# Second batch's sums over positions: from TensorE to VectorE, and two query loads issued earlier

## The chip, the cores and the metric

The kernel runs on one core of a Trainium2 chip. The metric is the device time of one execution in microseconds (us). A core has TensorE (PE, matrix multiply; its weight loads are shown apart as PEld), VectorE (DVE), ScalarE (ACT), GpSimd (POOL) and SyncE (SP), whose queue issues every load and store of this kernel. Each engine works through its own list of instructions in order, and waits where an instruction needs something from another engine or from a load.

## What is computed

An attention with keys and values that are averaged over groups of 8 positions, then two feed-forward layers over the 4608 tokens (8 batches of 576 positions; 8 heads of 64):

```
k_p = k.reshape(B, H, Sp, 8, D).mean(axis=3)      # 576 positions -> 72
v_p = v.reshape(B, H, Sp, 8, D).mean(axis=3)
attn = softmax(q @ k_p.T / sqrt(D));  x = attn @ v_p
h = x @ w_in;  x = (h * sigmoid(1.702 * h)) @ w_out       # 512 -> 2048 -> 512
out = ((x @ w_a) * (x @ w_b)) @ w_out2                    # 512 -> 1536 -> 512
```

The sums over 8 positions (the means, with the factor put elsewhere) are what the change moves.

## The kernel before, in words

**Tiling.** The 4608 tokens are 36 units of 128 tokens, and 9 blocks of 512 tokens (4 units each). A batch has 4.5 units, so units 0 to 3 need batch 0 alone, unit 4 needs batches 0 and 1, units 5 to 7 batch 1. Attention of a unit `u` has four stages: `stage_b1` (scores `sc` on PE from queries `q` and the block-diagonal keys `kbd`, maximum `mx` on DVE, exponentials `at` on ACT, in two halves), `stage_b2` (`sm`, `at` scaled, DVE), `stage_c` (transposes `pt` on PE, copied to `aT` by ACT) and `stage_d` (`px` = values times `aT` on PE, split into `xhi` on ACT, line 85, and `xlo` on DVE, line 86).

**Feed-forward.** Every large product is made of three matmuls of 512 columns (`mm3`, lines 130 to 132) on operands split in a high and a low part. One step of the first layer for a slice `f` of the hidden width is `emit_h` (12 matmuls into `h`; then `g` by ACT and DVE, `ghi` by ACT, `glo` by DVE, line 400) and `emit_y` (12 matmuls into `acc`). The weights of a slice are loaded raw (`raw`) and converted by DVE with ACT (`convert`, lines 108 to 127), in four parts for a slice.

**The start.** Block 0's attention (units 0 to 3) is written in a fixed DVE order by `in_order`, which puts each operation behind the newest DVE operation; the parts of the weights of slices 0 and 1 are placed between. Then come the first `FA` = 6 slices of layer 1 on block 0 (steps 0 to 5). Around them `filler` places, in a fixed DVE order too, the conversions of slices 2 to 5 and the attention of units 4 to 7 (the list `ahead_`). After these the loop over all remaining steps runs, with the later attention and weights spread over it.

**Where the sums are made.** Batch 0's: `sum_k` (line 194; DVE adds up, ACT writes `kbd` by `to_kbd`) and `sum_v` (line 214; DVE). Batch 1's: `sum_k_pe` (line 200) and `sum_v_pe` (line 219) on PE, as products with the identity matrix, 8 for each half, added up in PSUM (`ksp`, `vsp`); ACT writes `kbd` from `ksp`, and copies `vsp` to `vs` (line 229). Their places are lines 627 to 628 (keys, behind step 0's `emit_h`) and 635 to 637 (values, behind step 0's `emit_y`). Batches 2 and on use `sum_k` and `sum_v`.

**What sets the order.** On DVE the fixed order of `in_order`. On the other engines a scheduler orders the instructions when the program is built, by its own estimate of when the inputs are there. The loads of the start (lines 575 to 591) go out on SP in the order in which they are written; `qs` holds the queries of units 0 to 3, `kvraw` the keys and values of batches 0 and 1.

Of the kernel before, what the change touches and what calls it, by code (L numbers as in the profile page):

```python
# [9 lines left out]
F32 = mybir.dt.float32  # L10
# [6 lines left out]
POOL = 8  # L17
# [7 lines left out]
def tile_kernel(ctx, tc, q, k, v, w_in, w_out, w_a, w_b, w_o2, out):  # L25
# [13 lines left out]
    nc = tc.nc  # L39
    P = 128  # L40
    NU, _, NP, _ = q.shape
    B, SP, H, D, _ = v.shape
# [19 lines left out]
    ps = ctx.enter_context(tc.tile_pool(name="ps", bufs=4, space=bass.MemoryType.PSUM))  # L62
# [7 lines left out]
    def vec(made):  # L70
        newest[0] = made.ins
        return made

    def in_order(*ops):

        for o in ops:
            if newest[0] is None:
                o()
            else:
                with tc.issue_after(newest[0]):  # L80
                    o()
# [52 lines left out]
    ident = const.tile([P, P], F32, name="ident")  # L134
# [22 lines left out]
    ap_ = at.enter_context(tc.tile_pool(name="ap", bufs=1))  # L157
# [4 lines left out]
    q_t, ks_t, vs_t, at_t, atT_t, kraw_t, vraw_t = {}, {}, {}, {}, {}, {}, {}  # L162
# [10 lines left out]
    def load_q(u, t=None):  # L173
        q_t[u] = ap_.tile([P, NP, P], F32, tag="q", name="q", bufs=2) if t is None else t
        nc.sync.dma_start(out=q_t[u], in_=q[u])
# [11 lines left out]
    def to_kbd(b, half, ks):  # L187


        cs = slice(2 * half, 2 * half + 2)  # L190
        nc.scalar.mul(out=kbd[b % 2][0:D, cs, 0:SP], in_=ks[0:D], mul=scale)
        nc.scalar.mul(out=kbd[b % 2][D:P, cs, SP:2 * SP], in_=ks[D:P], mul=scale)
# [4 lines left out]
        vec(nc.vector.tensor_reduce(out=ks, in_=raw, op=ALU.add, axis=AX.X))  # L197
        to_kbd(b, half, ks)

    def sum_k_pe(b, half):  # L200

        ks = ps.tile([P, 2, SP], F32, tag="ps", name="ksp")
        raw = kraw_t.pop((b, half)).rearrange("p c (s r) -> p c s r", r=POOL)
        for r in range(POOL):
            nc.tensor.matmul(out=ks, lhsT=ident, rhs=raw[:, :, :, r], start=r == 0, stop=r == POOL - 1)
        to_kbd(b, half, ks)

    def load_v(b, h, n, raw=None):
        if raw is None:
            raw = ap_.tile([SP, n, D, POOL], F32, tag="vraw", name="vraw", bufs=2)  # L210
        nc.sync.dma_start(out=raw, in_=v[b, :, h:h + n])
        vraw_t[b, h] = raw

    def sum_v(b, h, n):
        if h == 0:
            vs_t[b] = ap_.tile([SP, H, D], F32, tag="vs", name="vs", bufs=2)
        vec(nc.vector.tensor_reduce(out=vs_t[b][:, h:h + n, :], in_=vraw_t.pop((b, h)), op=ALU.add, axis=AX.X))

    def sum_v_pe(b, h, n):

        if h == 0:
            vs_t[b] = ap_.tile([SP, H, D], F32, tag="vs", name="vs", bufs=2)
        raw = vraw_t.pop((b, h))
        vp = ps.tile([SP, n, D], F32, tag="ps", name="vsp")
        for r in range(POOL):
            nc.tensor.matmul(  # L226
                out=vp, lhsT=ident[:SP, :SP], rhs=raw[:, :, :, r], start=r == 0, stop=r == POOL - 1
            )
        nc.scalar.copy(out=vs_t[b][:, h:h + n, :], in_=vp)

    def stage_b1(u, half):
        qT = q_t[u]
# [68 lines left out]
    def op(f, *a):  # L301
        return lambda: f(*a)
# [30 lines left out]
    def as_words(t):  # L333
        return t.rearrange("p (f w) -> p f w", w=2)

    def sources(key):
        kind, f = key
        if kind == 1:
            return columns("in", f), rows("out", f)
        if kind == 2:  # L340
            return columns("a", f), columns("b", f)
        return rows("o2", 2 * f), rows("o2", 2 * f + 1)

    def load_w(key, raw=None, parts=(0, 1)):
        if raw is None:
            raw = wp.tile([P, 2, 1024], U32, tag="w", name="raw")
        raw_t[key] = raw
        for e, src in enumerate(sources(key)):
            if e not in parts:
                continue  # L350
            nc.sync.dma_start(out=as_words(raw[:, e]), in_=src)
# [29 lines left out]
    def emit_h(i, j, f):  # L381
        xhi, xlo = x_t[i, j]
        w = w_t[1, f]
        hps = ps.tile([P, N], F32, tag="ps", name="h")
        for kk in range(KD):
            cs = slice(kk * P, (kk + 1) * P)
            mm3(hps, w[:, 0, cs], w[:, 2, cs], xhi[:, kk, :], xlo[:, kk, :], kk == 0, kk == KD - 1)

        g = gp.tile([P, N], F32, tag="g", name="g", bufs=1)
        ghi = gp.tile([P, N], F32R, tag="ghi", name="ghi")  # L390
        glo = gp.tile([P, N], F32R, tag="glo", name="glo")
        nc.scalar.activation(out=g, in_=hps, func=AF.Tanh, scale=0.5 * 1.702)  # L392

        def rest():
            made = vec(nc.vector.scalar_tensor_tensor(out=g, in0=g, scalar=1.0, in1=hps, op0=ALU.add, op1=ALU.mult))  # L395
            nc.scalar.copy(out=ghi, in_=g)  # L396
            anchors[i, j, f] = made.ins
            g_t[i, j, f] = (ghi, glo)

        return rest, lambda: vec(nc.vector.tensor_tensor(out=glo, in0=g, in1=f32(ghi), op=ALU.subtract))  # L400
# [101 lines left out]
    def second(s):  # L502
        i, j, f = s
        layer, fs = passes[i]
        if f == fs[0]:
            sums[i, j] = [acc.tile([P, N], F32, tag="acc", name="acc") for _ in range(4)]
        (emit_y if layer == 1 else emit_o)(f, g_t.pop(s), sums[i, j], f == fs[0], f == fs[-1])
        if f == fs[-1]:
            finish(i, j, sums.pop((i, j)))
# [6 lines left out]
    for i in range(1, 4):  # L516
        fs = passes[i][1]
        for j in range(NB):
            n = place[i, j, fs[0]]
# [53 lines left out]
    qs = wp.tile([P, UB, NP, P], F32, tag="w", name="qs")  # L573
    kv0, kv1 = load_kv(0), load_kv(1)
    next(kv0)
    load_q(0, qs[:, 0])
    next(kv0)
    load_w((1, 0), parts=(0,))
    load_q(1, qs[:, 1])
    next(kv0)  # L580
    next(kv0)
    load_w((1, 0), raw_t[1, 0], (1,))
    load_q(2, qs[:, 2])
    load_q(3, qs[:, 3])
    load_w((1, 1))
    next(kv1)
    next(kv1)
# [4 lines left out]
    half_v = H // 2  # L592
# [20 lines left out]
    hs = {}  # L613

    def filler(n):

        for _ in range(n):
            if parts:
                f = FA - len(parts) // 4
                if len(parts) % 4 == 0 and f + 2 < FA:  # L620
                    load_w((1, f + 2))
                in_order(parts.pop(0))
            in_order(*ahead_[:per])
            del ahead_[:per]

    hs[0] = emit_h(*steps[0])
    for half in range(2):
        sum_k_pe(1, half)
    in_order(hs[0][0])
    filler(1)  # L630
    in_order(hs[0][1])
    for n in range(1, FA):
        hs[n] = emit_h(*steps[n])
        second(steps[n - 1])
        if n == 1:
            sum_v_pe(1, 0, half_v)
            sum_v_pe(1, half_v, half_v)
        filler(2)
        in_order(hs[n][0])
        filler(1)  # L640
        in_order(hs[n][1])
        filler(1)
# [61 lines left out]
```

## Time and profile before

| | |
|---|---|
| time, median of 3 runs | 1863.94 us (1863.19 to 1864.61) |
| the profiled execution | 1863.16 us, of which the span is 1861.4 us |
| PE busy | 1827.5 us (98% of the span) |
| DVE busy | 836.5 us (45%) |
| ACT busy | 549.6 us (30%) |
| mean granted TensorE clock | 0.985 of full |

The profiled execution spends 1.76 us outside its span (1863.16 - 1861.4). Busy shares are averages over stages with different limits: the first 138 us hold three stages (block 0's attention; steps 0 and 1 with the batch's sums; the conversions and units 4 to 7), and the rest is one long stage. So the profile is read by stretches of time. [...]

### The profile page before, as it was taken

Reading aid. Unit: us, or ns where it says so; the run is one execution under the profiler, and the core shown is the slowest. Engines: PE = TensorE matmul, PEld = TensorE weight load, DVE = VectorE, ACT = ScalarE, POOL = GpSimd, SP = SyncE. Lnnn points to the kernel's source line nnn. Section 1 sums busy time; section 2 is a strip of 40 time slices with the busy share of each in tenths; the row PEclk is TensorE's granted clock in tenths of the full one; section 3 lists DMA queues with packets and bytes.
Section 4 is the critical chain, followed back from the end, with each engine's and each line's share of the span. In section 5 each row is a group of like instructions: output and inputs, shape, how many; then the busy total and the mean of one; then the engine's idle time right before and its main releaser. Section 6 shows DMA issues by size and latency. Waiting matters only on the chain.

```text
span 1861.4 us, 21690 instructions
## 1 busy us (share of the span) xinstructions
PE 1827.5 (98%) x8656; PEld 1499.9 (81%) x8656; DVE 836.5 (45%) x1436; ACT 549.6 (30%) x1375; POOL 1.7 (0%) x8
## 2 busy tenths in 40 slices
PE   5989999999999999999999999999999999999998
PEld 4668888888888888888888888888888888888887
DVE  6496776656554354445444454455311221221222
ACT  5355555554332222323222222222111111111111
POOL 0000000000000000000000000000000000000000
PEclk8789999999999999999999999999999999999999
DMA  9154444324522223333324342432202211220200
GB/s 312 60 181 169 167 141 147 132 108 147 204 106 94 94 80 125 136 125 108 111 88 158 126 158 101 170 124 91 91 8 83 91 52 39 90 91 3 88 23 23
DMA packets 58614, 206.94 MB, mean 111 GB/s; under 512 B 6576, under 2 KB 6576, under 8 KB 46704
## 3 DMA queue, kind: packets, MB, share of 16 engines
q1 hardware_dynamic: 58512, 205.55, 31.0%
q8 instruction: 68, 1.11, 0.3%
q14 instruction: 34, 0.28, 0.0%
HBM read 139.46 MB, written 66.06 MB: 110 GB/s over the span
## 4 chain that ended last, share of the span: by engine, by line
PE 96%; DVE 2%; DMA 1%; ACT 1%; issue 0%; DVEq 0%; ACTq 0%
PE ab L132 11%; PE ab L130 11%; PE ab L131 11%; PE acc L130 7%; PE acc L131 7%; PE acc L132 7%; PE h L130 7%; PE h L131 7%; PE h L132 7%; PE acc L435 5%; PE acc L436 5%; PE acc L437 5%; PE px L289 2%; PE sc L244 2%; PE pt L276 2%; PE vsp L226 1%
## 5 line engine op out<-in xcount | busy, mean ns | idle before, releaser
L131 PE MATMUL ab<-xlo,w 128*128 128x512 f32 x864 | 336.2, 389 | 0.0
L132 PE MATMUL ab<-xhi,w 128*128 128x512 f32 x864 | 336.2, 389 | 0.0
L130 PE MATMUL ab<-xhi,w 128*128 128x512 f32 x864 | 336.2, 389 | 0.0
L423 DVE TENSOR_TENSOR c<-c,ab 128x512 f32<-128x512 f32 x108 | 74.2, 687 | 530.3 <-PE ab L132 530.3
L131 PE MATMUL acc<-glo,w 128*128 128x512 f32 x576 | 228.6, 397 | 0.0
L130 PE MATMUL h<-xhi,w 128*128 128x512 f32 x576 | 226.3, 393 | 0.7 <-ACT xhi L85 0.7
L132 PE MATMUL acc<-ghi,w 128*128 128x512 f32 x576 | 226.1, 393 | 0.0
L131 PE MATMUL h<-xlo,w 128*128 128x512 f32 x576 | 225.4, 391 | 0.0
L132 PE MATMUL h<-xhi,w 128*128 128x512 f32 x576 | 225.2, 391 | 0.0
L395 DVE SCALAR_TENSOR_TENSOR g<-g,h 128x512 f32<-128x512 f32 x144 | 98.5, 684 | 236.7 <-ACT g L392 236.3
L130 PE MATMUL acc<-ghi,w 128*128 128x512 f32 x576 | 188.8, 401 | 2.2 <-ACT ghi L396 2.2
L131 PEld LDWEIGHTS ab<-xlo,w 128*128 128x128 f32 x864 | 162.2, 188 | 33.7
L132 PEld LDWEIGHTS ab<-xhi,w 128*128 128x128 f32 x864 | 162.2, 188 | 33.7
L130 PEld LDWEIGHTS ab<-xhi,w 128*128 128x128 f32 x864 | 162.2, 188 | 33.5
L392 ACT ACTIVATE g<-h 128x512 f32<-128x512 f32 x144 | 86.1, 598 | 337.8 <-PE h L132 329.6
L422 ACT COPY c<-ab 128x512 f32<-128x512 f32 x108 | 63.4, 587 | 357.2 <-PE ab L132 357.2
L436 PE MATMUL acc<-w,chi 128*128 128x512 f32 x432 | 168.1, 389 | 0.0
L435 PE MATMUL acc<-w,chi 128*128 128x512 f32 x432 | 168.1, 389 | 0.0
L437 PE MATMUL acc<-w,clo 128*128 128x512 f32 x432 | 167.6, 389 | 0.0
L85 ACT CAST chi<-c 128x512 fp32r<-128x512 f32 x108 | 66.9, 620 | 288.5 <-DVE c L423 288.5
L130 PEld LDWEIGHTS h<-xhi,w 128*128 128x128 f32 x576 | 108.9, 189 | 24.1 <-ACT xhi L85 1.1
L131 PEld LDWEIGHTS acc<-glo,w 128*128 128x128 f32 x576 | 108.8, 189 | 23.4 <-issue 1.5
(68 smaller groups left out, 2094.1 us busy)
## 6 DMA issues: line engine op xcount, KB each, us to landing
part<-ys SPq DMA_DIRECT2D x72, 256.0 KB
part<-part SPq DMA_DIRECT2D x18, 1024.0 KB
xhi<-yd SPq DMA_DIRECT2D x18, 1024.0 KB
xlo<-yd SPq DMA_DIRECT2D x18, 1024.0 KB
xd<-xhi SPq DMA_DIRECT2D x9, 1024.0 KB
xd<-xlo SPq DMA_DIRECT2D x9, 1024.0 KB
xhi<-xd SPq DMA_DIRECT2D x9, 1024.0 KB
xlo<-xd SPq DMA_DIRECT2D x9, 1024.0 KB
```

The costliest lines, as they stand in the source:

```text
L85: nc.scalar.copy(out=hi, in_=src)
L130: nc.tensor.matmul(out=o, lhsT=whi, rhs=xhi, start=first, stop=False)
L131: nc.tensor.matmul(out=o, lhsT=whi, rhs=xlo, start=False, stop=False)
L132: nc.tensor.matmul(out=o, lhsT=wlo, rhs=xhi, start=False, stop=last)
L244: nc.tensor.matmul(out=sc[o:o + n, 2 * c:2 * c + 2, :].rearrange("p h k -> p (h k)"), lhsT=qT[:, pair, o:o + n], rhs=kbd[b % 2][:, pair, : ...
L392: nc.scalar.activation(out=g, in_=hps, func=AF.Tanh, scale=0.5 * 1.702)
L395: made = vec(nc.vector.scalar_tensor_tensor(out=g, in0=g, scalar=1.0, in1=hps, op0=ALU.add, op1=ALU.mult))
L422: nc.scalar.copy(out=cc, in_=pab[0])
L423: made = nc.vector.tensor_tensor(out=cc, in0=cc, in1=pab[1], op=ALU.mult)
L435: nc.tensor.matmul(out=o, lhsT=chi[:, cs], rhs=whi, start=first, stop=False)
L436: nc.tensor.matmul(out=o, lhsT=chi[:, cs], rhs=wlo, start=False, stop=False)
L437: nc.tensor.matmul(out=o, lhsT=clo[:, cs], rhs=whi, start=False, stop=last)
```

## The change

`sum_k_pe` and `sum_v_pe` go away. Batch 1's key sums are made by `sum_k` on DVE, both ahead of step 0's `g`, and its value sums by `sum_v` on DVE, behind step 0's `glo`; all four stand in the fixed DVE order. Among the first loads, the queries of unit 1 go ahead of the first part of slice 0's weights, those of unit 2 ahead of batch 0's values, and those of unit 3 ahead of the second part of slice 0's weights.

```diff
-    def sum_k_pe(b, half):
-        ks = ps.tile([P, 2, SP], F32, tag="ps", name="ksp")
...
-            nc.tensor.matmul(out=ks, lhsT=ident, rhs=raw[:, :, :, r], start=r == 0, stop=r == POOL - 1)
-        to_kbd(b, half, ks)
-    def sum_v_pe(b, h, n):
...
-        nc.scalar.copy(out=vs_t[b][:, h:h + n, :], in_=vp)
...
     load_q(0, qs[:, 0])
     next(kv0)
+    load_q(1, qs[:, 1])
     load_w((1, 0), parts=(0,))
-    load_q(1, qs[:, 1])
+    load_q(2, qs[:, 2])
     next(kv0)
     next(kv0)
+    load_q(3, qs[:, 3])
     load_w((1, 0), raw_t[1, 0], (1,))
-    load_q(2, qs[:, 2])
-    load_q(3, qs[:, 3])
     load_w((1, 1))
...
     hs[0] = emit_h(*steps[0])
-    for half in range(2):
-        sum_k_pe(1, half)
-    in_order(hs[0][0])
+    in_order(op(sum_k, 1, 0), op(sum_k, 1, 1), hs[0][0])
     filler(1)
-    in_order(hs[0][1])
+    in_order(hs[0][1], op(sum_v, 1, 0, half_v))
...
         if n == 1:
-            sum_v_pe(1, 0, half_v)
-            sum_v_pe(1, half_v, half_v)
+            in_order(op(sum_v, 1, half_v, half_v))
```

The order of the built programs, at three places (with the tiles' numbers; behind the removed functions line numbers are 20 lower, so L254 of before is L234 of the change, L85 stays).

ACT at the start of block 0, before: `kbd` of batch 0, then slice 0's first conversion (L108) ahead of the exponentials of unit 0 (`at_169`).

```order
L191 ACTIVATE kbd0_122<-ks_165 64x2x72
L192 ACTIVATE kbd0_122<-ks_165 64x2x72
L108 ACTIVATE tmp_126<-raw_134 128x512
L254 ACTIVATE at_169,sm_171<-sc_172,mx_170 128x72 x4
L119 CAST w_180<-tmp_126 128x512
L254 ACTIVATE at_169,sm_171<-sc_186,mx_170 128x72 x4
```

ACT at the same place, of the change:

```order
L191 ACTIVATE kbd0_122<-ks_165 64x2x72
L192 ACTIVATE kbd0_122<-ks_165 64x2x72
L234 ACTIVATE at_169,sm_171<-sc_172,mx_170 128x72 x4
L108 ACTIVATE tmp_126<-raw_135 128x512
L119 CAST w_180<-tmp_126 128x512
L234 ACTIVATE at_169,sm_171<-sc_186,mx_170 128x72 x4
```

The conversion's first instruction has moved behind the four exponentials.

ACT in the second half of block 0 (unit 1's `px_306` becomes `xhi`; slice 1's second conversion begins with L108; unit 3's exponentials are `at_278`), before:

```order
L277 COPY aT_293<-pt_300 72x512
L254 ACTIVATE at_278,sm_280<-sc_281,mx_279 128x72 x4
L85 CAST xhi_265<-px_306 128x4x128
L108 ACTIVATE tmp_127<-raw_144 128x512
L254 ACTIVATE at_278,sm_280<-sc_317,mx_279 128x72 x4
```

ACT at the same place, of the change:

```order
L257 COPY aT_293<-pt_300 72x512
L234 ACTIVATE at_278,sm_280<-sc_281,mx_279 128x72 x4
L108 ACTIVATE tmp_127<-raw_144 128x512
L85 CAST xhi_265<-px_306 128x4x128
L234 ACTIVATE at_278,sm_280<-sc_317,mx_279 128x72 x4
```

The conversion's L108 now stands ahead of `xhi` of unit 1.

DVE from the end of slice 1's conversion (L127 of `w_330`) over step 0's `g` and `glo` to unit 5's first maximum, before:

```order
L127 TENSOR_TENSOR w_330<-tmp_127,raw_144 128x512
L395 SCALAR_TENSOR_TENSOR g_415<-g_415,h_402 128x512
...
L251 TENSOR_REDUCE mx_453<-sc_465 128x4
L400 TENSOR_TENSOR glo_417<-g_415,ghi_416 128x512
L122 TENSOR_SCALAR raw_151<-tmp_126 128x512
...
L127 TENSOR_TENSOR w_446<-tmp_126,raw_151 128x512
L251 TENSOR_REDUCE mx_539<-sc_541 128x4
```

DVE at the same place, of the change:

```order
L127 TENSOR_TENSOR w_330<-tmp_127,raw_144 128x512
L197 TENSOR_REDUCE ks_419<-kvraw_147 128x144
L197 TENSOR_REDUCE ks_423<-kvraw_149 128x144
L375 SCALAR_TENSOR_TENSOR g_415<-g_415,h_402 128x512
...
L231 TENSOR_REDUCE mx_439<-sc_451 128x4
L380 TENSOR_TENSOR glo_417<-g_415,ghi_416 128x512
L209 TENSOR_REDUCE vs_466<-kvraw_154 72x256
L209 TENSOR_REDUCE vs_466<-kvraw_156 72x256
L122 TENSOR_SCALAR raw_151<-tmp_126 128x512
...
L127 TENSOR_TENSOR w_432<-tmp_126,raw_151 128x512
L231 TENSOR_REDUCE mx_507<-sc_509 128x4
```

The four sums stand in DVE's row ahead of `g` and behind `glo`; the other rows keep their places.

## Rows read from the trace of the kernel before

**Rows 1.** Busy time by stretch: from:to, length, then each engine's busy us (instructions).

```profile
41.00:77.00 36.00, 35.99 (x122) 23.58 (x123) 9.10 (x17) 8.07 (x28) 0.00 (x0) 0.78 0.28 108
77.00:138.00 61.00, 51.43 (x289) 39.97 (x288) 56.31 (x102) 35.75 (x132) 0.00 (x0) 0.81 0.45 148
138.00:1861.00 1723.00, 1718.17 (x8120) 1419.98 (x8120) 741.92 (x1268) 481.44 (x1126) 0.00 (x0) 1.00 0.29 105
```

**Rows 2.** Chain of waits that ended last, 0 to 160 us: start, us, what.

```profile
41.80 5.23 PE ksp L205 x20
...
47.28 0.23 PE h L132
...
49.55 3.13 PE ksp L205 x12
52.68 0.88 PE sc L244 x10
...
58.09 11.19 PE vsp L226 x24
...
69.70 0.43 PE acc L132
...
72.68 3.67 PE vsp L226 x8
...
124.18 9.47 DMA kraw<-in_k_dram
```

**Rows 3.** Timeline of DVE, 41 to 78 us: start, us, instruction [idle before, releaser].

```profile
43.37 0.69 DVE L127 TENSOR_TENSOR w<-tmp,raw 128x512 fp32r<-128x512 f32 x1
50.22 0.69 DVE L395 SCALAR_TENSOR_TENSOR g<-g,h 128x512 f32<-128x512 f32 x1 [6.15 <-ACT g L392]
...
51.74 0.69 DVE L116 SCALAR_TENSOR_TENSOR tmp<-raw,tmp 128x512 uint32<-128x512 uint32 x1
...
58.50 0.68 DVE L400 TENSOR_TENSOR glo<-g,ghi 128x512 fp32r<-128x512 f32 x1
...
60.88 0.69 DVE L127 TENSOR_TENSOR w<-tmp,raw 128x512 fp32r<-128x512 f32 x1
76.88 0.46 DVE L251 TENSOR_REDUCE mx<-sc 128x4 f32<-128x288 f32 x1 [15.31 <-PE sc L244]
```

**Rows 4.** Batch 0's sums and key copies, by tile: ns min/median/max, first and last start.

```profile
L191 ACT ACTIVATE kbd<-ks x14: 306/323/330, 7.7 to 324.0; 64x144 f32<-64x144 f32 x14
L197 DVE TENSOR_REDUCE ks<-kvraw x2: 1352/1353/1354, 5.0 to 8.4; 128x144 f32<-128x1152 f32 x2
...
L217 DVE TENSOR_REDUCE vs<-kvraw x2: 2273/2274/2275, 16.2 to 19.5; 72x256 f32<-72x2048 f32 x2
```

**Rows 5.** Busy time by stretch, PE's granted clock behind POOL's column: steps 0 and 1.

```profile
42.00:46.00 4.00, 4.00 (x17) 4.00 (x16) 2.00 (x4) 0.67 (x1) 0.00 (x0) 0.50 1.02 423
46.00:62.00 16.00, 16.00 (x68) 10.61 (x68) 5.98 (x11) 6.10 (x24) 0.00 (x0) 1.00 0.33 117
```

**Rows 6.** Timeline of ACT and DVE at the start of block 0, 10 to 13 us.

```profile
11.07 0.30 ACT L254 ACTIVATE at<-sc,mx 128x72 f32<-128x72 f32 x1
11.19 0.43 DVE L111 TENSOR_SCALAR tmp<-tmp 128x512 f32<-128x512 f32 x1 [0.90 <-ACT tmp L108]
...
12.16 0.21 ACT L254 ACTIVATION_READ_ACCUMULATOR at<-sc,mx 128x1 f32 x1
```

**Rows 7.** Timeline of PE, ACT and DVE later in block 0, 17 to 31 us.

```profile
17.50 2.26 PE L244 MATMUL sc<-kbd,qs 128*128 128x144 f32 x8 [3.73 <-DMA qs<-in_q_dram]
...
19.74 1.89 PE L276 MATMUL pt<-ident,at 128*72 128x128 f32 x8
...
29.62 0.58 ACT L85 CAST xhi<-px 128x512 fp32r<-128x512 f32 x1 [0.58 <-PE px L289]
30.10 0.67 ACT L108 ACTIVATE tmp<-raw 128x512 f32<-128x512 f32 x1
...
30.23 0.69 DVE L86 TENSOR_TENSOR xlo<-px,xhi 128x512 fp32r<-128x512 f32 x1 [0.39 <-ACT xhi L85]
```

More of the change, by code (lines that the diff above doesn't have):

```diff
@@ L198, in sum_k @@
         to_kbd(b, half, ks)
-    def sum_k_pe(b, half):
-        ks = ps.tile([P, 2, SP], F32, tag="ps", name="ksp")
-        raw = kraw_t.pop((b, half)).rearrange("p c (s r) -> p c s r", r=POOL)
-        for r in range(POOL):
-            nc.tensor.matmul(out=ks, lhsT=ident, rhs=raw[:, :, :, r], start=r == 0, stop=r == POOL - 1)
-        to_kbd(b, half, ks)
     def load_v(b, h, n, raw=None):
@@ L217, in sum_v @@
         vec(nc.vector.tensor_reduce(out=vs_t[b][:, h:h + n, :], in_=vraw_t.pop((b, h)), op=ALU.add, axis=AX.X))
-    def sum_v_pe(b, h, n):
[L221 to L228, printed above, removed]
-        nc.scalar.copy(out=vs_t[b][:, h:h + n, :], in_=vp)
     def stage_b1(u, half):
```

## The prediction

> **What bounds the kernel now.** I read busy time by stretch first [rows 1]. From 138 us to the end PE is busy in 1718.2 of 1723 us at full clock: PE alone sets that stretch, the change leaves its work alone, and it simply starts when PE gets there. So what counts is how early PE arrives at the point that is 138 us now. Before it lie two stretches of another kind. From 41 to 77 us PE is busy all the time and DVE in only 9.1 of 36 us. From 77 to 138 us it is the other way round: DVE is busy in 56.3 of 61 us, and PE is idle for 9.6.
>
> The chain of waits [rows 2] says what PE does from 41 to 77 us: batch 1's key sums take 5.23 + 3.13 = 8.36 us of the chain, its value sums 11.19 + 3.67 = 14.86 us, together 23.2 us. The timeline of DVE [rows 3] shows who waits: DVE stands for 6.15 us until step 0's `g`, and for 15.31 us until unit 5's first maximum at 76.88 us, whose scores are queued on PE behind the value sums. From that maximum on DVE is full. So 76.88 us is the mark: when DVE gets to this maximum in the changed kernel, and whether the 61 us behind it keep their length.
>
> **Block 0: the loads and ACT's order.** The queries of unit 2 were waited for: PE stood 3.73 us until 17.50 us [rows 7]. This is no gain: the scores of unit 2 then run 2.26 us, end at 19.76, and the transposes that follow them start at 19.74, back to back, as soon as DVE has unit 0's `at`; and the maximum of unit 2 stands on DVE behind both value sums of batch 0. I take 0 (at best 0.1 us). What the loads do change is ACT's row. At the start its first conversion, L108, now stands behind four exponentials instead of ahead of them. They run from 11.07 to 12.16 + 0.21 = 12.37 us, 1.3 us [rows 6], and by so much L108 comes later. DVE waited for just this instruction (0.90 us of idle until 11.19), and its row is fixed: it is 1.3 us later from there on. Later in block 0 L108 now goes ahead of unit 1's `xhi`. L108 has to wait for DVE's work that ends 0.39 us before 30.23, at 29.84 us; with its own 0.67 us, `xhi` starts at about 30.45 instead of 29.62, and the `xlo` behind it, for which DVE already waits, comes 0.8 us later [rows 7]. Nothing that is late behind it hides this: the transposes of unit 2 wait for DVE. Sum for block 0: **+2.1 us**, with bounds of 0 (the first conversion's weights or another release come last, so the order costs nothing) and +3 (PE's scores and products there run at the lower clock for longer).
>
> **Key sums.** DVE is free at 43.37 + 0.69 = 44.06 us [rows 3] (I keep the old times and add the 2.1 us at the end). One sum is 1.35 us, then ACT makes two copies of 0.32 us before the one `ks` tile is free, then the second sum of 1.35 us [rows 4]: DVE is free for `g` at 47.5 us. On PE the 11 remaining matmuls of step 0's `h` start where `ksp` did, at 41.8. Each takes 0.23 us at the full clock and 0.43 at half [rows 2]. The clock was at half from 42 to 46 us and full behind it [rows 5], and I take it to rise no sooner: 11 x 0.43 = 4.7, so `h` ends at 46.5, ACT's `g` at about 47.2, and DVE's `g` starts at 47.5. The key sums lie in the idle 6.15 us of DVE and cost nothing there; if that cover were gone, they would cost 2.7 us.
>
> **From `g` to the mark.** `g` and three conversion steps take 51.74 + 0.69 - 50.22 = 2.2 us: 49.7. PE meanwhile does step 1's `h`, 12 x 0.23 = 2.8 us (49.3), and the scores of unit 4, 0.9 us [rows 2]: 50.2. Two maxima of 0.46 us each: 51.2. Then `glo`, the two value sums (2 x 2.27 = 4.5 us) and the second half of a conversion; `glo` and that conversion took 60.88 + 0.69 - 58.50 = 3.1 us before. 51.2 + 4.5 + 3.1 = 58.8 us, and with block 0's 2.1 us the mark is at **60.9 us instead of 76.88: 16.0 us earlier**. Queued behind the value sums are the conversion and unit 5's maximum, and PE waits for the latter: its eight `acc` matmuls end some 2 us behind `glo`, about 54 us, and it then stands for some 6 us until unit 4's scaled `at`. That pause is what the 4.5 us of value sums cost, and it is inside the 16.0.
>
> The bounds: with the clock at half up to here, `h` of step 1 is 12 x 0.43 = 5.2 us and the scores double, 3.3 us later, so 12.7 us are gained. With the clock full from 41.8, `g` still waits for the key sums at 47.5, so 16.0 stays, and with nothing lost in block 0 it is 18.1.
>
> [...]
>
> **Behind the mark.** DVE's row up to what is now about 128 us is the same, instruction by instruction, so the 61 us move along. ACT's row differs in places (some `ghi` and `g` earlier), which can move single waits. All idle of DVE there is 61 - 56.3 = 4.7 us, the most that could be gained; I take 0 and allow 3 either way. The loads move with DVE: the one in the chain at 124.18 us (9.47 us) [rows 2] is issued when a key sum frees its tile.
>
> **The sum.** Against the profiled execution: 1863.16 - 16.0 = 1847.2 us. The median before is 0.8 us above the profiled one; I put the forecast between, at **1847.5 us**. With the bounds 12.7 and 18.1 and the 3 us behind the mark, the forecast's own range is a gain of 10 to 21 us.
>
> **The rivals.**
> 1. *The clock stays low and gives part back.* Behind the mark, PE comes out of a pause of 6 us where it was busy without a break. Each `h` or `acc` block of 12 matmuls that runs at half clock and is waited for costs 12 x 0.20 = 2.4 us. Four such blocks are 9.6 us: a gain of 6.4, **1857 us**. For it: the mean granted clock is only 0.81 from 77 to 138 us, with PE idle in places [rows 1]. Against it: there DVE, not PE, is full.
> 2. *The clock stays low throughout: slower.* Steps 1 to 5 have 5 x 24 = 120 `h` and `acc` matmuls by the code; with a mean clock of 0.81 today [rows 1] the clock is at half for 0.19 / 0.5 = 38% of the time, and I take some 90 not to be at half. 80 of these at half clock on the path (80 x 0.20 = 16 us) eat the whole gain; that is the point from which this decides. All 90 are 18 us, the 3.3 us of the bound above come on top, and the scores of four units at twice their 0.9 us [rows 2] some 4: 16.0 - 25 = -9, **1872 us**. Against it: the clock was back at full within the first steps, at 46 us, while PE ran without a gap [rows 5]. [...]
> 3. *Another thing sets the mark at 138 us: no change.* If the loads around 124 us did not move with DVE, the gain would wait there: **1862 us**. Against it: that load's own issue waits for DVE. That the change does not do what it says can be excluded by the built order for the sums; for the queries it is my forecast that they bring nothing.
> 4. *More than forecast.* Block 0 costs nothing, and the waits among the 4.7 us behind the mark go too: 18.1 + 4.7 = 22.8, **1840 us**.
>
> **How the numbers follow.** Forecast 0.65, rival 1 0.16, rival 2 0.07, rival 3 0.06, rival 4 0.06. A measurement of this kernel tells about 0.2% (3.7 us) from no change. Forecast, rival 1 and rival 4 are faster: 0.87. Rival 3 is the same: 0.06. Rival 2 is slower: 0.07. The range leaves out rivals 2 and 3 and the outer parts of rivals 1 and 4, 0.2 in all: gains from 6 to 22 us, 1841 to 1857.5.
>
> **What would show it.** Right: no `ksp` or `vsp` on PE; L111 at about 12.5 instead of 11.19 us; unit 1's `xlo` 2 us later than 30.23; the key sums on DVE without a wait for PE, `g` behind them with nearly none; unit 5's first maximum near 61 us, right behind the conversion's L127; a pause of PE of some 6 us before unit 4's transposes; the end of the DVE stretch near 122 us, and PE full from there. Wrong, and in which step: the maximum at 61 us but PE's full stretch not earlier by as much (behind the mark: clock or loads); L111 at 11.2 (block 0's price); half the granted clock through the `h` of steps 1 and 2 (rival 1 or 2); DVE waiting for PE's scores ahead of `glo` (the upper bound of the middle).

## The result and the profile after

| | before | changed |
|---|---|---|
| time, median (lowest to highest, runs) | 1863.57 us (1862.56 to 1864.61, 4) | 1848.12 us (1846.80 to 1848.59, 4) |
| the profiled execution | 1863.16 us, span 1861.4 us | 1848.59 us, span 1846.8 us |
| PE busy | 1827.5 us | 1807.4 us |
| PE idle in the span | 33.9 us | 39.4 us |
| DVE busy | 836.5 us | 843.7 us |

The ratio is 0.9916, with a 95% interval from 0.9899 to 0.9933: 15.5 us faster by the medians, 14.6 us by the profiled executions. The forecast was 1847.5 us. The shortest reading of the gain is in the rows on PE: its busy time fell by 20.1 us (1827.5 - 1807.4; the sums that left it had 23.2 us of the chain, [rows 2]), and 5.5 us came back as idle time (39.4 - 33.9). 20.1 - 5.5 = 14.6 us.

Busy time by stretch of the changed kernel (from:to, length, then busy us of PE, PEld, DVE, ACT and POOL, the granted clock, DMA share, GB/s), beside [rows 1]:

```profile
41.00:77.00 36.00, 28.01 (x164) 21.61 (x162) 31.85 (x50) 20.54 (x74) 0.00 (x0) 0.84 0.39 145
77.00:138.00 61.00, 54.97 (x283) 41.39 (x279) 52.55 (x92) 33.12 (x117) 0.00 (x0) 0.86 0.56 181
138.00:1846.00 1708.00, 1702.76 (x8039) 1407.90 (x8036) 730.89 (x1250) 473.00 (x1098) 0.00 (x0) 1.00 0.29 105
```

The stretch from 41 to 77 us has turned over. Before, PE was busy in all of it and DVE in 9.1 us; now DVE is busy in 31.85 of 36 us and PE waits for it. The long stretch behind is as it was, but shorter.

The timeline of DVE in the changed kernel (start, us, instruction, idle before and its releaser), beside [rows 3, 6, 7]:

```profile
12.52 0.43 DVE L111 TENSOR_SCALAR tmp<-tmp 128x512 f32<-128x512 f32 x1 [2.11 <-ACT tmp L108]
...
32.38 0.69 DVE L86 TENSOR_TENSOR xlo<-px,xhi 128x512 fp32r<-128x512 f32 x1 [1.20 <-ACT xhi L85]
...
46.12 1.35 DVE L197 TENSOR_REDUCE ks<-kvraw 128x144 f32<-128x1152 f32 x1
48.25 1.35 DVE L197 TENSOR_REDUCE ks<-kvraw 128x144 f32<-128x1152 f32 x1 [0.78 <-ACT kbd L192]
...
50.34 0.69 DVE L375 SCALAR_TENSOR_TENSOR g<-g,h 128x512 f32<-128x512 f32 x1 [0.74 <-ACT g L372]
...
54.57 4.47 DVE L209 TENSOR_REDUCE vs<-kvraw 72x256 f32<-72x2048 f32 x2
...
60.73 0.69 DVE L127 TENSOR_TENSOR w<-tmp,raw 128x512 fp32r<-128x512 f32 x1
61.34 0.45 DVE L231 TENSOR_REDUCE mx<-sc 128x4 f32<-128x288 f32 x1
```

Each step can be read off here. The first conversion comes at 12.52 instead of 11.19 us, unit 1's `xlo` at 32.38 instead of 30.23. The two key sums stand where DVE used to wait 6.15 us, `g` is ready 0.74 us behind them, and the value sums follow `glo`. Unit 5's first maximum, the mark, starts at 61.34 us with no idle time ahead of it, where it had waited 15.31 us until 76.88.

The timeline of PE in the changed kernel, in the same columns:

```profile
48.61 0.59 PE L130 MATMUL h<-xhi,w 128*128 128x512 f32 x1
49.03 0.40 PE L131 MATMUL h<-xlo,w 128*128 128x512 f32 x1
...
63.04 1.89 PE L256 MATMUL pt<-ident,at 128*72 128x128 f32 x8 [5.55 <-DVE at L248]
...
103.58 1.92 PE L256 MATMUL pt<-ident,at 128*72 128x128 f32 x8 [1.21 <-DVE at L248]
```

The first two rows are the tenth and eleventh matmul of step 0's `h`, where the clock rises: up to there they begin 0.43 us apart, behind it 0.24. The pause of 5.55 us is the one that the prediction priced at some 6. The last row is PE's last wait of over a microsecond; from there it runs to the end almost without a gap. In the kernel before it is this row of PE's timeline:

```profile
118.45 1.92 PE L276 MATMUL pt<-ident,at 128*72 128x128 f32 x8 [1.74 <-DVE at L268]
```

So this wait, and not the round 138 us of the prediction, is where PE takes over. It came 14.87 us earlier (118.45 - 103.58), the span shrank by 14.6. The same holds in every profiled execution of this study:

| kernel | unit 5's first maximum | DVE idle between | PE's last wait over 1 us ends | span | span less that |
|---|---|---|---|---|---|
| before | 76.88 | 2.19 | 118.45 | 1861.4 | 1743.0 |
| changed | 61.34 | 2.92 | 103.58 | 1846.8 | 1743.2 |
| changed, second profile (e5) | 61.43 | 0.50 | 101.14 | 1843.2 | 1742.1 |
| changed, third profile (e12) | 60.06 | 2.42 | 101.99 | 1844.1 | 1742.1 |
| old loads (e1) | 58.66 | 1.84 | 99.79 | 1842.6 | 1742.8 |
| old loads, second profile (e9) | 58.80 | 1.89 | 99.99 | 1842.2 | 1742.2 |
| new loads alone (e2) | 79.27 | 0.67 | 119.34 | 1862.3 | 1743.0 |
| keys alone (e3) | 71.78 | 1.40 | 112.63 | 1855.5 | 1742.9 |
| values alone (e4) | 68.04 | 1.74 | 109.08 | 1851.7 | 1742.6 |
| short values (e6) | 58.30 | 5.76 | 103.43 | 1845.2 | 1741.8 |
| values on GpSimd (e7) | 60.58 | 2.87 | 102.66 | 1844.4 | 1741.7 |
| half the values on PE (e8) | 63.38 | 1.71 | 104.32 | 1846.3 | 1742.0 |
| values later (e10) | 56.30 | 6.77 | 106.84 | 1848.2 | 1741.4 |
| busy PE (e11) | 58.96 | 0.42 | 98.81 | 1842.1 | 1743.3 |

(In e10 the value sums stand behind the first maximum, so its second column isn't to be compared.) The last column stays within 1.9 us while the spans differ by 20. Up to these 1.9 us, what a variant does to the time is what it does to the end of that wait, and the rest of this text asks for that.

The column on DVE's idle time splits the way to that end. From the maximum to the end of PE's last wait, less DVE's idle time between them, it is 39.2 to 39.5 us in thirteen profiles (before: 118.45 - 76.88 - 2.19 = 39.4), and 39.3 in e10 when its 4.47 us of value sums are taken off. So a profile differs from another by two things only: when DVE gets to the mark, and how long it waits behind it. Those waits are two in the main, for one `xlo` (0 to 2.81 us) and for one load of values (0.42 to 3.20 us).

### The profile page after: what moved, and what is told of

It reads as the page before. It is cut to its first block, busy times and chain, and to the rows that moved or that the text cites. A ratio compares the mean times of both kernels' runs of the same rounds, so it can differ in the third digit from the quotient of the medians.

```text
span 1846.8 us, 21557 instructions
## 1 busy us (share of the span) xinstructions
PE 1807.4 (98%) x8592; PEld 1487.3 (81%) x8592; DVE 843.7 (46%) x1440; ACT 549.4 (30%) x1373; POOL 1.7 (0%) x8
## 4 chain that ended last, share of the span: by engine, by line
PE 95%; DVE 3%; ACT 1%; DMA 1%; issue 0%; DVEq 0%; ACTq 0%
PE ab L130 11%; PE ab L131 11%; PE ab L132 11%; PE h L130 7%; PE h L131 7%; PE h L132 7%; PE acc L130 7%; PE acc L131 7%; PE acc L132 7%; PE acc L415 5%; PE acc L416 5%; PE acc L417 5%; PE px L269 2%; PE sc L224 2%; PE pt L256 2%; DVE vs L209 1%
## 5 line engine op out<-in xcount | busy, mean ns | idle before, releaser
L85 ACT CAST chi<-c 128x512 fp32r<-128x512 f32 x108 | 66.9, 620 | 288.8 <-DVE c L403 288.8
L131 PEld LDWEIGHTS h<-xlo,w 128*128 128x128 f32 x576 | 109.6, 190 | 23.4 <-issue 0.4
```

What stands on the lines that cost most here:

```text
L85: nc.scalar.copy(out=hi, in_=src)
L131: nc.tensor.matmul(out=o, lhsT=whi, rhs=xlo, start=False, stop=False)
```

## The experiments

The theory is the prediction's: PE's sums were on the path, DVE's are in its idle time (keys) or cost a pause (values), and block 0 costs 2.1 us. The rivals are in the expectations. (The new order of the loads moves the queries of three units, 1, 2 and 3, not of two as the title has it.)

**The sums without the new loads (e1, e9), and the change again beside it (e5, e12).** e1 and e9 are the changed kernel with the loads in the old order:

```diff
     next(kv0)
-    load_q(1, qs[:, 1])
     load_w((1, 0), parts=(0,))
-    load_q(2, qs[:, 2])
+    load_q(1, qs[:, 1])
     next(kv0)
     next(kv0)
-    load_q(3, qs[:, 3])
     load_w((1, 0), raw_t[1, 0], (1,))
+    load_q(2, qs[:, 2])
+    load_q(3, qs[:, 3])
```

> The sums on VectorE as in the change, the first loads in the order of the kernel before (ScalarE's row in block 0 is then the old one too). Theory: the new order of the loads costs 2.1 us in block 0 (1.3 us by the first L108 behind the exponentials, 0.8 us by the L108 ahead of unit 1's xhi) and gains nothing: 1848.1 - 2.1 = 1846.0 us, with L111 at 11.2 us instead of 12.5 and unit 5's first maximum near 59.2 instead of 61.3 us. Rival, the loads bring something (the wait of 3.73 us for unit 2's queries): slower than the change, 1849 to 1852 us. Rival, block 0 is hidden behind something else: 1848.1 us, the same.

> The changed kernel once more, beside three variants. Theory (block 0's new order of loads costs 2 to 4 us, which the first experiment with the old order gave as 1844.25): 1848 us again, 3 to 4 us above that version. Rival (the distance came from the day): within 1 us of 1844 to 1845.

> The change's sums with the old order of the loads once more, beside the change in the same stretch. Theory: block 0's order costs 2.1 us at unit 1's xlo and all of it reaches the end: 2 us below the change. Rival A: given back behind: 0. Rival B: about 4 us as between the first runs of the two (1848.1 and 1844.25).

> The changed kernel beside the one with the old loads: by the theory 2 us above it, about 1846.5 us; by rival A the same, by rival B 4 us above it.

Measured: old loads 1844.25 us (1842.82 to 1844.85; ratio to the kernel before 0.9896, 0.9884 to 0.9909) and 1844.98 us (1843.98 to 1845.80; 0.9896, 0.9881 to 0.9910). The change 1846.15 us (1844.97 to 1847.35; 0.9910, 0.9896 to 0.9923) and, in the same stretch as e9, 1845.94 us (1845.86 to 1847.04; 0.9903, 0.9886 to 0.9919). The pair from one stretch (e12, e9) says 1 us, between the theory and "given back"; the first two (1848.12 and 1844.25) say 3.9, but come from different stretches, and e5 lies between its two expectations. The mean of all 12 runs of the change is 1846.75 us, that of all 8 with the old loads 1844.49: 2.3 us, with an uncertainty of about 1 us by the spread of the runs, which come from stretches in which the kernel before had medians from 1862.74 to 1863.91 us. The trace of e1, timeline of DVE and then PE, and behind it ACT's in the change:

```profile
10.71 0.43 DVE L111 TENSOR_SCALAR tmp<-tmp 128x512 f32<-128x512 f32 x1 [0.90 <-ACT tmp L108]
...
29.63 0.69 DVE L86 TENSOR_TENSOR xlo<-px,xhi 128x512 fp32r<-128x512 f32 x1 [0.17 <-ACT xhi L85]
...
99.79 1.92 PE L256 MATMUL pt<-ident,at 128*72 128x128 f32 x8 [2.43 <-DVE at L248]
```

```profile
11.81 0.67 ACT L108 ACTIVATE tmp<-raw 128x512 f32<-128x512 f32 x1
...
31.21 0.66 ACT L108 ACTIVATE tmp<-raw 128x512 f32<-128x512 f32 x1 [0.85 <-DVE w L127]
31.77 0.57 ACT L85 CAST xhi<-px 128x512 fp32r<-128x512 f32 x1
```

DVE waits for L108 for 0.90 us here and 2.11 in the change. That is the exponentials' place in ACT's row, 1.2 us: L108 starts right behind them at 11.81, without a wait. Measured from batch 0's second key sum to block 0's last `xlo` on DVE, block 0 takes 32.56 us before, 32.43 and 32.12 with the old loads, and 34.59, 35.04 and 34.57 in the three profiles of the change. The other profiles agree: 35.01 to 35.04 with the new loads (e2, e3, e4, e6), 32.29 and 32.30 with the old ones (e8, e11), and one exception, 33.83 in e10 (in e7 GpSimd lengthens the block, see there). In e10, and in e5 and the four with 35.01 to 35.04, unit 1's `xhi` waits last for PE's `px`, which takes 1.12 us there instead of 0.66 in e9, as at half clock; so at half clock the order costs 1.2 us (35.04 - 33.83), and otherwise 2.0 to 2.5. Whether the new order makes the half clock likelier (five of seven profiles against one of six) stays open. So the sums alone are the better kernel: faster than the change, and than the kernel before by 18.5 and 18.9 us against its medians in the same stretches.

**The new loads without the sums (e2).** The edit is the other half of the diff: the kernel before, with its sums on PE, and the loads as in the change.

> The kernel before with only the new order of the first loads; the sums stay on TensorE. Theory: 1863.6 + 2.1 = 1865.7 us, step 0's first matmul near 43.1 instead of 41.0 us, unit 5's first maximum near 79.0. Rival, the loads bring something: 1860 to 1863 us. Rival, hidden: 1863.6 us.

Measured: 1863.96 us (12 runs) against 1862.74 (21 runs), ratio 1.0004 (0.9995 to 1.0013), which is 0.7 us with an interval of -0.9 to +2.4 (the medians are 1.2 us apart). The time can't tell 2.1 us from nothing. The timeline of DVE can, up to the mark; behind it a row of the kernel before:

```profile
79.27 0.46 DVE L251 TENSOR_REDUCE mx<-sc 128x4 f32<-128x288 f32 x1 [15.44 <-PE sc L244]
```

```profile
106.12 0.69 DVE L86 TENSOR_TENSOR xlo<-px,xhi 128x512 fp32r<-128x512 f32 x1 [1.39 <-ACT xhi L85]
```

The mark is 2.4 us later than 76.88, and 1.5 us of that are gone again at PE's last wait (119.34 against 118.45). They are idle time of DVE: the kernel before waits 1.39 us for this `xlo` and 0.16 us for a maximum, e2 for neither. Why this `xlo` is late in the one and not in the other stays open; the theory's 2.1 us are inside the interval.

**One pair of sums at a time (e3, e4).** e3 leaves the value sums on PE, e4 the key sums; both have the new loads.

```diff
 e3
-    in_order(hs[0][1], op(sum_v, 1, 0, half_v))
+    in_order(hs[0][1])
...
-            in_order(op(sum_v, 1, half_v, half_v))
+            sum_v_pe(1, 0, half_v)
+            sum_v_pe(1, half_v, half_v)
 e4
-    in_order(op(sum_k, 1, 0), op(sum_k, 1, 1), hs[0][0])
+    for half in range(2):
+        sum_k_pe(1, half)
+    in_order(hs[0][0])
```

> The change with the value sums still on TensorE: only the key sums go to VectorE. Theory (VectorE's arrival at unit 5's first maximum counts, and the key sums lie in its idle time): TensorE reaches the value sums 6.6 us earlier, since 8.4 us of key sums go and step 0's h runs longer at half clock; with the 2.1 us of block 0 the gain is 4.5 us: 1859.1 us, the maximum near 72.4 us. Rival (TensorE's work counts, every us taken from it is gained): 8.4 us, 1855.2 us.

> The change with the key sums still on TensorE: only the value sums go to VectorE. Theory: VectorE ends the conversion behind glo at 61.57 us today; with 4.5 us of value sums ahead of it and 2.1 us of block 0 the maximum is near 68.2 instead of 76.88 us, a gain of 8.7: 1854.9 us. Rival (every us taken from TensorE is gained): 14.9 us, 1848.7 us.

Measured: keys alone 1858.4 us, ratio 0.9975 (0.9966 to 0.9984); values alone 1853.48 us, ratio 0.9945 (0.9933 to 0.9957). Both lie within 1.5 us of the theory and 3 to 5 us from the rival, which counted each sum's PE time in full. But the rival's prices leave out block 0's 2.1 us, which the theory's have; with them it forecasts gains of 6.3 and 12.8 us, and the measured ones have intervals of 3.0 to 6.3 and 8.0 to 12.5, so the two times alone hardly exclude it. All four sums together do, where block 0 costs nothing: 23.2 us by the rival against 18.5 and 18.9 in e1 and e9. And DVE's row shows the mechanism, in e3, and then in e4:

```profile
71.78 0.46 DVE L251 TENSOR_REDUCE mx<-sc 128x4 f32<-128x288 f32 x1 [15.15 <-PE sc L244]
```

```profile
52.39 0.69 DVE L395 SCALAR_TENSOR_TENSOR g<-g,h 128x512 f32<-128x512 f32 x1 [6.16 <-ACT g L392]
...
60.29 0.46 DVE L251 TENSOR_REDUCE mx<-sc 128x4 f32<-128x288 f32 x1 [4.30 <-PE sc L244]
...
68.04 0.45 DVE L251 TENSOR_REDUCE mx<-sc 128x4 f32<-128x288 f32 x1
```

Each pair of sums on PE leaves its own holes in DVE's row: 15.15 us with the values there; 6.16 us ahead of `g`, and 0.94 and 4.30 us ahead of unit 4's two maxima, with the keys there. (The kernel before has all of them: 6.15, 0.94, 4.30 and 15.31 us.)

**What the value sums cost on DVE (e6).** Batch 1's value sums are made over one position of 8.

```diff
+        vec(nc.vector.tensor_reduce(out=vs_t[b][:, h:h + n, :], in_=raw[:, :, :, 0:1], op=ALU.add, axis=AX.X))
```

> The change, with batch 1's value sums over one position of 8 (seven eighths of these sums are left out). Theory: from step 0's glo on DVE's row sets when PE becomes full, so the two sums of 2.27 us cost their length: 4.5 x 7/8 = 4 us less, about 1844 us. Rival: they lie in a pause that PE has anyway (it waits for ACT, for loads, or runs at half clock behind the pause): within 1 us of the change, about 1848 us.

Measured: 1843.52 us (1842.40 to 1847.00; 0.9899, 0.9884 to 0.9913), 2.6 us less than the change beside it (1846.15, 1844.97 to 1847.35; the ranges overlap). The 4 us of the expectation were too much: the two short sums take 1.23 us where the full ones take 4.47, so 3.2 us are taken out, and the mark, at 58.30, is 3.1 us earlier than in e5. Up to the mark DVE's row gives all of it back. Behind it the profiled execution, the longest of the four runs, loses it again: PE's last wait ends at 103.43 instead of 101.14. DVE's and SP's timelines (on SP's queue the second number is the time an issue takes):

```profile
54.77 1.23 DVE L215 TENSOR_REDUCE vs<-kvraw 72x256 f32<-72x256 f32 x2
...
101.25 1.22 DVE L209 TENSOR_REDUCE vs<-vraw 72x128 f32<-72x1024 f32 x1 [3.20 <-DMA vraw<-in_v_dram]
...
94.81 0.33 SPq L284 DMA_DIRECT2D xd<-xhi  x1
95.19 0.39 SPq L203 DMA_DIRECT2D vraw<-in_v_dram  x1
```

The load in the chain of waits (start, us, what), of e6 and then of the change:

```profile
95.19 6.04 DMA vraw<-in_v_dram
```

```profile
96.05 3.19 DMA vraw<-in_v_dram
```

DVE is done with one sum over this tile by 91.83 + 1.20 = 93.03 us, and the tile could be refilled, but in SP's row a store of `xhi` (1024 KB) that is issued only at 94.81 stands ahead of the load. The load is issued at 95.19, 2.2 us late, and then takes 6.04 us instead of 3.19. In the change the load goes first (SP issues it at 96.05, the store at 98.03), and DVE waits 0.42 us (0.50 in e5) instead of 3.20. The rest is a wait of 2.56 us for an `xlo`, which e5 doesn't have (see the part behind the mark below): -3.1 + 2.7 + 2.6 = 2.2 us, of the 2.3 by which PE's last wait ends later.

The sums were shortened and nothing else, so it is the scheduler's estimate of them that turned the order on SP. The same order, store ahead of load, stands in e3, e7, e8 and e10: from the issue of the load to the sum over it there are 6.0 to 6.1 us in all five, and DVE waits 1.40, 2.87, 1.71 and 1.67 us in the four. In the nine other profiles the load goes first, it is 3.2 to 3.5 us, and DVE waits 0.42 to 0.75. So each of the five variants changes two things, and its time can't be put down to its edit alone.

**The value sums on GpSimd (e7).** With the old loads, batch 1's value sums are made by GpSimd, as three additions of halves for each of the two tiles.

```diff
+        for w in (4, 2):
+            nc.gpsimd.tensor_tensor(out=raw[:, :, :, 0:w], in0=raw[:, :, :, 0:w], in1=raw[:, :, :, w:2 * w], op=ALU.add)
+        nc.gpsimd.tensor_tensor(
+            out=vs_t[b][:, h:h + n, :], in0=raw[:, :, :, 0], in1=raw[:, :, :, 1], op=ALU.add
+        )
```

> Old order of loads (1844.25 us with the sums on DVE), batch 1's value sums on GpSimd, which does nothing after the start. Theory: DVE's row loses 4.5 us, so 1840 us, as long as the sums are done before unit 4's product needs them (some 10 us behind step 0's glo). Rival A: GpSimd takes longer than that and PE waits for it: 1844 us or more. Rival B: DVE's instructions get longer while GpSimd works: DVE groups beside it show more than 0.69 us, 1842 to 1848 us.

Measured: 1846.12 us (1844.77 to 1846.87; 0.9909, 0.9895 to 0.9922), some 1.5 us slower than with the sums on DVE (1844.25, 1844.98, in other stretches; the intervals of the ratios overlap). Rival B, by the trace. The timelines of GpSimd and of DVE:

```profile
32.30 7.62 POOL L216 TENSOR_TENSOR kvraw<-kvraw 72x1024 f32<-72x1024 f32 x4 [30.00 <-DMA kvraw<-in_v_dram]
39.89 1.77 POOL L217 TENSOR_TENSOR vs<-kvraw 72x256 f32<-72x256 f32 x2
...
32.52 2.58 DVE L111 TENSOR_SCALAR tmp<-tmp 128x512 f32<-128x512 f32 x1
35.13 2.45 DVE L112 TENSOR_SCALAR tmp<-tmp 128x512 uint32<-128x512 uint32 x1
37.62 1.41 DVE L116 SCALAR_TENSOR_TENSOR tmp<-raw,tmp 128x512 uint32<-128x512 uint32 x1
...
47.29 0.69 DVE L86 TENSOR_TENSOR xlo<-px,xhi 128x512 fp32r<-128x512 f32 x1 [1.17 <-ACT xhi L85]
...
100.49 1.22 DVE L209 TENSOR_REDUCE vs<-vraw 72x128 f32<-72x1024 f32 x1 [2.87 <-DMA vraw<-in_v_dram]
```

GpSimd is free, so the sums start as soon as their load is in, inside block 0. Beside them DVE's L111 takes 2.58 us instead of 0.43, L112 2.45 instead of 0.43, L116 1.41 instead of 0.69, and block 0's last `xlo` comes at 47.29 instead of 40.4 to 40.7 us. DVE saves 4.5 us behind `glo` and has lost some 6.7 in block 0 by then (6.3 of it in these three instructions and three more beside GpSimd's); what is left, 2 us, is the distance of the marks (60.58 against 58.66). PE's last wait ends 2.9 us later (102.66 against 99.79): the load behind the store, as in e6, adds 2.4 us of waiting to e1's 0.45, and e1's wait of 1.39 us for an `xlo` is missing. That GpSimd takes 9.4 us for the sums (7.62 + 1.77) against 4.47 on DVE shows up in no wait; what it does to its neighbour costs the 2 us at the mark.

**Half of the value sums on PE (e8).** With the old loads, the second half's sum goes to PE, into the pause.

```diff
-            in_order(op(sum_v, 1, half_v, half_v))
+            sum_v_pe(1, half_v, half_v)
```

> Old order of loads, key sums and the first half of the value sums on DVE, the second half on PE, which has a pause of 5.5 us there. Theory: DVE's row loses 2.3 us, PE's half (14.86 / 2 = 7.4 us) fills the pause: 1842 us if only DVE counts. Rival: the PE sums come ahead of unit 5's scores and delay the mark by 7.4 - 5.5 = 1.9 us: 1844 to 1846 us.

Measured: 1847.95 us (1846.14 to 1848.26; 0.9916, 0.9902 to 0.9929), some 3 us slower than the old loads alone. The timeline of DVE:

```profile
63.38 0.46 DVE L240 TENSOR_REDUCE mx<-sc 128x4 f32<-128x288 f32 x1 [6.13 <-PE sc L233]
```

The rival's mechanism, at more than its price: PE's products stand ahead of step 0's `acc` and unit 5's scores, DVE waits 6.13 us for those, and the mark moves from 58.66 to 63.38. (PE's last wait ends 4.5 us later than in e1; in it the load behind the store has 1.3 us more, and e1's 1.39 us for an `xlo` are missing.) PE had a pause, but not at the place in its row where the sum was written.

**The value sums later on DVE (e10).** With the old loads, both sums move behind unit 4's scaled `at`. DVE's row keeps its length, and PE's order is unchanged.

```diff
+    def scaled_then_sums(scaled):
+        return lambda: in_order(scaled, op(sum_v, 1, 0, half_v), op(sum_v, 1, half_v, half_v))
+    at4 = len(later[UB]) + 1
+    ahead_[at4] = scaled_then_sums(ahead_[at4])
```

> Old order of the loads; both value sums moved on DVE behind unit 4's scaled at, so that PE's pause of 5.5 us ahead of unit 4's transposes goes, while DVE's row keeps its length. Theory (DVE's row sets PE's last wait): within 1 us of the version with the old loads, about 1844.5 us. Rival (PE's pause is the price, by its idle time or the clock behind it): 2 to 4.5 us less, 1840 to 1842.5 us.

Measured: 1848.61 us (1846.60 to 1849.95; 0.9914, 0.9900 to 0.9929), 3.6 us slower than e9 in the same stretch. Neither side was right. The one pause of PE is gone, and in its place there are six stops of 0.2 to 1.5 us between 57 and 70 us, 6.0 us together: the pause is split up, and PE's idle time did not go. Busy time by stretch, 62 to 77 us, of e9 and then of e10:

```profile
62.00:77.00 15.00, 12.12 (x98) 9.72 (x96) 14.59 (x29) 11.56 (x41) 0.00 (x0) 0.95 0.27 76
```

```profile
62.00:77.00 15.00, 11.60 (x45) 8.82 (x46) 14.26 (x26) 9.47 (x36) 0.00 (x0) 0.54 0.17 57
```

The clock (the figure behind GpSimd's 0.00) is at 0.95 behind the one long pause and at 0.54 with the many short ones, and PE gets 45 matmuls done in 11.6 us instead of 98 in 12.1 (of several sizes). DVE then waits for PE, as e10's timeline of DVE and PE shows:

```profile
78.89 0.46 DVE L231 TENSOR_REDUCE mx<-sc 128x4 f32<-128x288 f32 x1 [2.29 <-PE sc L224]
...
93.47 0.69 DVE L86 TENSOR_TENSOR xlo<-px,xhi 128x512 fp32r<-128x512 f32 x1 [2.81 <-ACT xhi L85]
...
104.67 1.22 DVE L209 TENSOR_REDUCE vs<-vraw 72x128 f32<-72x1024 f32 x1 [1.67 <-DMA vraw<-in_v_dram]
...
106.84 1.92 PE L256 MATMUL pt<-ident,at 128*72 128x128 f32 x8 [2.77 <-DVE at L248]
```

Block 0 was 1.4 to 1.7 us longer in this one execution (33.83 us against 32.43 and 32.12), so of the 6.9 us by which PE's last wait ends later than in e9 some 5 are made here: 2.29 us of waiting for scores that e9 doesn't have, 1.4 us more for this `xlo` (1.39 in e9), 1.2 us more for a load of values (1.67 against 0.50). The last is the store ahead of the load, as in e6, and hasn't to do with PE. The first two, 3.7 us, are the prediction's first rival at work: half clock where PE keeps stopping, and DVE waiting for it. So e10 shows what half clock can cost here; it doesn't show what the pause costs.

**PE kept busy (e11).** With the old loads, 20, 6 and 8 matmuls whose result nobody reads are put ahead of the transposes of units 4, 5 and 6.

```diff
+    def busy(n, o):
+        def run():
+            t = ps.tile([P, N], F32, tag="ps", name="busy")
+            for r in range(n):
+                nc.tensor.matmul(out=t, lhsT=w_t[1, 0][:, 0, 0:P], rhs=x_t[0, 0][0][:, 0, :], start=r == 0, stop=r == n - 1)
+            o()
+        return run
```

> Old order of the loads; PE's pauses ahead of the transposes of units 4, 5 and 6 are filled with 20, 6 and 8 matmuls of 512 columns whose result nobody reads. If the half clock behind pauses costs time: the h of step 3 and the transposes run at full clock and 1 to 3 us are gained, 1841.5 to 1843.5 us. If not: 1844.5 us, or up to 2 us more where the filling ends late.

Measured: 1844.08 us (1842.05 to 1846.92; 0.9892, 0.9877 to 0.9907), 0.9 us less than e9; the ranges overlap, and the time settles nothing. The trace shows the effect on the clock. Busy time from 77 to 90 us, of e9 and then of e11, and e11's timeline of PE:

```profile
77.00:90.00 13.00, 11.99 (x57) 9.09 (x58) 11.37 (x21) 6.89 (x25) 0.00 (x0) 0.74 0.20 69
```

```profile
77.00:90.00 13.00, 12.18 (x72) 9.32 (x72) 12.58 (x24) 8.62 (x31) 0.00 (x0) 1.00 0.32 95
...
54.85 4.81 PE L599 MATMUL busy<-xhi,w 128*128 128x512 f32 x20
...
98.81 1.92 PE L256 MATMUL pt<-ident,at 128*72 128x128 f32 x8 [1.52 <-DVE at L248]
```

The granted clock is 1.00 instead of 0.74, DVE is busy 1.2 us more of the 13, and PE's last wait ends at 98.81 instead of 99.99. In this execution the span gave it back again (1842.1 against 1842.2). So about 1 us may hang on the clock there, which is less than the spread of the runs.

## Why the prediction was right, step by step

**PE alone sets the time behind a point, and what counts is when it gets there: right.** The table above is that statement in numbers. The point was put too late: 138 us was the edge of a stretch that I had chosen, PE's last wait of over 1 us ended at 118.45. As nothing between the two decides, no number hung on it.

**Block 0, +2.1 us: right.** L111 at 12.5 was forecast and is at 12.52; unit 1's `xlo` is 2.15 us later (32.38 - 30.23, forecast 2.1). The queries are no longer waited for, and that brought nothing, as forecast. The three profiles of the change have block 0 2.0 to 2.5 us longer than before, and the time differs by 2.3 us over all runs. It is the one part of the change that makes the kernel slower than it was. In the first and the third profile both places are in ACT's row, as forecast, and not in the transfers; in e5 PE's lower clock has the last word at the second, which the forecast had as its upper bound.

**Key sums free, `g` behind them: right.** `g` was forecast at 47.5 + 2.1 = 49.6 us and is at 50.34. The 0.74 us are a wait for ACT's `g`, and the step that was off is PE's order: I had unit 4's scores behind step 1's `h`, but four of them run between the first and the second matmul of step 0's `h`. The chain of waits of the changed kernel (start, us, what):

```profile
43.94 1.15 PE sc L224 x4
45.10 0.73 PE h L131
```

That is 1.15 us that the sum didn't have. It counts only while the clock is at half: in e12 PE's matmuls of `h` begin 0.23 us apart from 46.7 us on, not from 49.0, and `g` follows the key sums without a wait (timeline of DVE in e12):

```profile
49.34 0.68 DVE L375 SCALAR_TENSOR_TENSOR g<-g,h 128x512 f32<-128x512 f32 x1
```

That is where the mark of e12, 60.06, gets most of its lead over 61.34. Keys alone gave 4.7 us by the ratio, with block 0's price in it (e3).

**The mark at 60.9 instead of 76.88: right within 0.9 us** (61.34; 61.43 and 60.06 in the other two profiles). The trace of the change has 1.35 us for a key sum and 4.47 for two value sums, as [rows 4], 7.2 us in all (2 x 1.35 + 4.47); the keys lie in DVE's idle time, and in e6 3.2 us less of value sums bring the mark 3.1 us forward. So only the value sums' part of the 7.2 us moves the mark, and on PE the same sums cost 23.2 us [rows 2].

**PE's pause of some 6 us: right** (5.55). That it "is what the 4.5 us of value sums cost" is too simple: e10 splits the pause up, with the same sums in DVE's row, and gets slower.

**Behind the mark, 0 with 3 either way: right in the sum, and half of the reason.** From the mark to PE's last wait it is 41.6 us before and 42.2, 39.7 and 41.9 in the three profiles of the change. That DVE's row "is the same, instruction by instruction, so the 61 us move along" holds for what DVE does there, 39.2 to 39.5 us in every profile. It doesn't hold for its waits, 0.42 to 2.92 us in these four: they come and go with the clock, and in the variants with the order on SP. The same program in two executions, timeline of PE and DVE of the first profile of the change, and then of e5:

```profile
84.77 0.80 PE L130 MATMUL h<-xhi,w 128*128 128x512 f32 x1
...
90.12 0.66 PE L269 MATMUL px<-aT,vs 72*64 72x128 f32 x8
...
91.45 0.69 DVE L86 TENSOR_TENSOR xlo<-px,xhi 128x512 fp32r<-128x512 f32 x1 [2.50 <-ACT xhi L85]
```

```profile
84.36 0.50 PE L130 MATMUL h<-xhi,w 128*128 128x512 f32 x1
...
87.35 0.66 PE L269 MATMUL px<-aT,vs 72*64 72x128 f32 x8
```

One `h` block of 12 matmuls takes 90.12 - 84.77 = 5.35 us in the one and 2.99 in the other, 2.4 us apart, and DVE waits 2.50 us for the `xlo` behind it in the one and, as its timeline shows no idle time there, not in the other. Between them lie e12 (the block takes 4.96 us, the wait is 1.67) and e1 (3.86 and 1.39). That is rival 1's price to the tenth (12 x 0.20 = 2.4 us); its count was four blocks, and here it is one, a part of one or none. The first profiled execution of the change, 1848.59 us, was one with the block at half; whether its three companions were isn't known, but their median, 1848.12, is the highest of three for this kernel (1846.15, 1845.94). So the forecast of 1847.5 lies inside the spread of what was measured, 1845.9 to 1848.1, and its closeness to the first of them is partly luck.

**The rivals.** The clock (1) exists and costs one block (2.4 us); in e10 it costs more (3.7 us), so it was rightly the largest rival. Slower throughout (2) falls: in the 15 us from 62 us on the granted clock is 0.72 to 0.89 in the three profiles of the change, so it is at half for a part, not throughout. No change (3) falls in its form, since the load of the old 124.18 us moves with DVE (it is issued at 109.06); in e6 another load does hold the end. More than forecast (4) comes half true with the old loads: 18.5 and 18.9 us in e1 and e9, with block 0 at nothing (18.1 in the prediction); the 4.7 us of waits behind the mark are not gained beside it.

**What stays open.** Why the kernel before waits 1.39 us for an `xlo` behind the mark and e2 doesn't; what sets the clock in block 0 and in the block behind the mark; and what e3, e6, e7, e8 and e10 would take with the load ahead of the store, which wasn't tried.

## What to carry to other kernels

Find the last long wait of the engine that is full afterwards, and judge each edit by when that wait ends; work moved from the full engine to one that is idle just there was worth here its length minus the new pause and what block 0 lost, and a change in an untouched engine's row (here two places on ACT) took some 2 us of it back. PE's pause was not filled by work that stood at another place in its row (e8: the mark at 63.38 instead of 58.66), and the idle engine was no free one where the busy one's instructions got longer beside it (e7: L111 2.58 us instead of 0.43). A variant built to change one thing can turn the order of a queue as well, so compare the waits in the trace, and the order on every engine, before the medians.

## What the hardware showed that I had not expected

**GpSimd's additions slowed DVE, and by form.** In e7 DVE's L111 and L112 (one input, 0.43 us alone) take 2.58 and 2.45 us beside GpSimd's additions, L116 (two inputs) 1.41 instead of 0.69. GpSimd's first four additions take 7.62 us, 1.9 each in the mean, and L111 is longer by 2.15 us, about the length of one addition. What holds DVE up there no run shows. Each form was met once or twice, in one profile.

**The load of values took almost twice as long behind the store of `xhi`.** It needs 6.0 to 6.1 us from its issue to the sum that waits for it where the store of `xhi` (1024 KB) goes out right ahead of it (five profiles), and 3.2 to 3.5 us where the load goes out first (nine). SP's row is not one of those that the edits touch, and it moved DVE's wait by 1 to 2.7 us.

**Six short stops did not keep the clock up.** With one pause of 5.55 us the clock is 0.72 to 0.95 from 62 to 77 us in the five profiles of the change and of the old loads (0.95 in e9, above); with six stops of 0.2 to 1.5 us, 6.0 us together, it is 0.54 (e10, one profile, and its four runs are slower too). I had taken the length of the longest pause as the danger, and e10 speaks against that. That short stops cost more than a long one isn't shown: e12, with the one pause, is at 0.50 from 62 to 70 us as well.

**In e5 the granted clock of the profile missed a slow stretch.** It reads 1.00 from 43 to 49 us, while the matmuls of step 0's `h` begin 0.43 us apart there, as at half; in e12 it reads 0.70 for the same 6 us, and they begin 0.43 and then 0.23 us apart. From 0 to 41 us e5 reads 1.00 too, with PE busy for 23.94 us in 120 matmuls, where the first profile of the change reads 0.76, with 21.63 us in 118. The starts of equal matmuls are the safer reading here.
